# Starting addresses of matmul operands in SBUF: an FFT filter and a gated network on one core

## The chip, the core and the metric

The kernel runs on one core of a Trainium2 chip. A core has TensorE (matmuls; in the profile PE, and PEld for the loading of weights into its array), VectorE (DVE), ScalarE (ACT), GpSimd (POOL) and SyncE (SP), which here only issues DMAs. The engines compute on SBUF, a memory of 128 partitions in which an address is a byte within a partition, and TensorE writes its sums to PSUM. Data outside the core lies in HBM and is moved by 16 DMA engines. The metric is the time of one execution on the device in microseconds (us); lower is better.

## The reference

For 8 batches of 3136 x 256 the sequence axis is filtered through a real FFT, and the result goes through a small network with a gate:

```python
X = np.fft.rfft(x, axis=1)
Y = X * (filt_r + 1j * filt_i)[None]
y = np.fft.irfft(Y, n=3136, axis=1)               # (8, 3136, 256)
h = np.maximum(y @ w_in, 0.0)                     # w_in: 256 x 1024
hp = pad(h, one row of zeros before and behind)
conv_out = conv_w[0] * hp[0:S] + conv_w[1] * hp[1:S+1] + conv_w[2] * hp[2:S+2]
out = (h * sigmoid(conv_out)) @ w_out             # w_out: 1024 x 256
```

All inputs and the output are float32 or float64 on the host; the kernel computes in float32.

## The kernel before

The kernel has two stages, and each writes down by hand in which order its instructions go to TensorE, ScalarE, VectorE and GpSimd.

The first stage is the FFT filter. It is built of matmuls with tables (steps `first`, `second`, `filt`, `third`), and between the steps the data goes out to HBM and comes back in another order (`a_dram`, `b_dram`). It runs for all eight batches in one loop.

The second stage begins with the last step of the inverse transform, `last_stage` (line 216): four small matmuls with the table `m2_sb`, whose results `last_out` writes into the y tiles of the batch. y is kept transposed, the 256 channels in two groups of 128 partitions (KT = 2 rows of a tile) and the 3136 positions along the row, with one zero column before and one behind. To keep the precision of float32 in a faster matmul format (`F32R`), each value is split into a high part and a low part: `hi_act` (line 146, ScalarE) writes the rounded value, and `lo_dve` (line 149, VectorE) what is left of it. So each batch has two y tiles, y0 (high) and y1 (low), and each tile has two rows. Tiles of even batches come from the pool `y_even` at the right end of SBUF, those of odd batches from `y_odd` on the left. While the network runs on one batch, `last_stage` and `last_out` of the next batch are spread between its steps in 14 pieces.

The network runs in units. A chunk is 896 positions, halved into two parts of 448; for each of 28 chunks, of eight groups of 128 hidden channels (f) and of two halves (i) there is one unit, 448 in all:

- `inner` makes the hidden values of 450 positions (448 and a neighbour on either side). For each of the two rows `mm3` issues three matmuls: high weight by high value (line 177), high by low (178), low by high (179). The weights `wi[0]`, `wi[1]` are loaded into the array, and a window of the y row streams through. That makes six matmuls of 450 columns.
- `relu`, `conv`, `gate`, `split_g` (ScalarE, VectorE, GpSimd) take ReLU, the convolution over three positions and the gate, and split the result into two parts, g0 and g1.
- `project` multiplies g with `wo`: here g is loaded as weights, 128 positions at a time, and 256 columns of `wo` stream (lines 475 to 477), three matmuls for each of the chunk's seven groups of 128 positions: 12 matmuls for one half, 9 for the other.
- `evacuate` brings finished sums to `ot`, and SyncE issues their DMA.

Within a pool tiles lie one behind another, each beginning at a multiple of 32 bytes. Pools of the left side are stacked upwards, those of the right side (`side="right"`) downwards. The pool `wc` is the first on the left: it holds `m2_sb`, `cw` (the convolution's weights, 3 x 8 values for each partition), `wi0`, `wi1`, `wo0`, `wo1`. When the second stage begins, the first stage's tiles are given up, and `y_even`, `lp` (the inputs `br` of the last transform step), `y_odd` and `wp` (t, g, ot) are laid over them. A tile so placed waits for the last reader of the tile that lay there (`reuse_waits="tile"`).

Of the kernel before, what the change touches and what calls it, by code (L numbers as in the profile page):

```python
# [9 lines left out]
F32 = mybir.dt.float32  # L10
F32R = mybir.dt.float32r
# [5 lines left out]
S = 3136  # L17
# [5 lines left out]
KT = D // 128  # L23
NF = FF // 128
SUB = 448
NSUB = S // SUB
CH = 2 * SUB
NT = CH // 128


def _k1(g, s):
# [93 lines left out]
def tile_fft_filter_gated_ffn(  # L125
# [58 lines left out]

    wc = ctx.enter_context(tc.tile_pool(name="wc", bufs=1))
    m2_sb = wc.tile([112, N1], F32, name="m2_sb")
    cw = wc.tile([128, 3, NF], F32, name="cw")
    nc.gpsimd.memset(cw[:, 0, 0:1], 0.0)
    nc.scalar.activation(cw[:, 0, 0:1], cw[:, 0, 0:1], AF.Sigmoid)
    wi = [wc.tile([128, KT, FF], F32R, name=f"wi{h}") for h in range(2)]  # L190
# [3 lines left out]
    ys, yps = {}, []  # L194
# [6 lines left out]

    def y_slices(b, sl):
        if sl.start == 0:
            ys[b] = [yps[b % 2].tile([128, KT, S + 2], F32R, name=f"y{h}") for h in range(2)]
            for t in ys[b]:
                nc.gpsimd.memset(t[:, :, 0:1].bitcast(F32), 0.0)
                nc.gpsimd.memset(t[:, :, S + 1:S + 2].bitcast(F32), 0.0)
        return (t[:, :, 1:S + 1].rearrange("p k (a c) -> p k c a", c=N2)[:, :, sl] for t in ys[b])
# [19 lines left out]
    with (  # L228
# [17 lines left out]
        def load_filter(c):  # L246
            for e in (4 * c, 4 * c + 2):
                nc.sync.dma_start(out=t1_sb[0:64, e:e + 2], in_=fr[:, e:e + 2])
                nc.sync.dma_start(out=t2_sb[56:120, e:e + 2], in_=fi[:, e:e + 2])

        def copy_filter(c):
            sl = slice(4 * c, 4 * c + 4)
            nc.scalar.activation(t1_sb[64:120, sl], t1_sb[0:56, sl], AF.Copy)
            nc.scalar.activation(t2_sb[0:56, sl], t2_sb[64:120, sl], AF.Copy)
            if c == 6:
                nc.sync.dma_start(out=t1_sb[92:93, G - 1], in_=nyq)
# [3 lines left out]
        def load_weights(k):  # L260
            raws[k] = raw = cv.tile([128, 2, 512], I32, name="raw")
            for part, src in enumerate((w_in, w_out)):
                nc.sync.dma_start(out=raw[:, part], in_=src[:, 512 * k:512 * k + 512])
# [34 lines left out]
        def load(kind, b, p):  # L298
            r = pool(kind).tile([112, 2, D], F32, name=kind, bufs=8 if kind == "x" else 5)
            if kind == "x":  # L300
                v = x[b].rearrange("(p n) d -> p n d", n=N2)
            else:
                v = a_dram[b].rearrange("n (r g) d -> (n r) g d", g=G)
            nc.sync.dma_start(out=r, in_=v[:, 2 * p:2 * p + 2])
            rows[kind, b, p] = r

        def store(kind, b, p, ps):
            st = pool(kind).tile([112, 2, D], F32, name=kind, bufs=4)
            nc.scalar.activation(st, ps, AF.Copy)  # L309
            sl = slice(2 * p, 2 * p + 2)  # L310
            if kind == "sa":
                v = a_dram[b][sl].rearrange("n p d -> p n d")
            else:
                v = b_dram[b].rearrange("n (r g) d -> (n r) g d", g=G)[:, sl]
            nc.sync.dma_start(out=v, in_=st)

        def first(b, p):
            r = rows.pop(("x", b, p))
            ps = fps.tile([112, 2, D], F32, name="ps")
            for j in range(2):  # L320
                nc.tensor.matmul(ps[:, j], lhsT=s1_sb[:, 2 * p + j], rhs=r[:, j], start=True, stop=True)  # L321
            return ps

        def second(b, p):
            r = rows.pop(("a", b, p))
            pp = fps.tile([120, 2, D], F32, name="pp", bufs=3)
            if p < NP - 1:
                nc.tensor.matmul(pp, lhsT=s2_sb, rhs=r, start=True, stop=True)  # L328
            else:
                for j, m in ((0, s2_sb), (1, s2s_sb)):  # L330
                    nc.tensor.matmul(pp[:, j], lhsT=m, rhs=r[:, j], start=True, stop=True)
            psums[b, p] = pp

        def filt(b, p):


            pp, v = psums.pop((b, p)), turned[p % 2]
            sl = slice(2 * p, 2 * p + 2)
            u = fp.tile([120, 2, D], F32, name="u", bufs=3)
            nc.vector.tensor_mul(u, pp, t1_sb[:, sl])  # L340
            nc.vector.tensor_mul(v[64:120], pp[0:56], t2_sb[0:56, sl])
            nc.vector.scalar_tensor_tensor(out=v[0:56], in0=pp[64:120], scalar=-1.0, in1=t2_sb[64:120, sl], op0=ALU.mult, op1=ALU.mult)  # L342
            z = fp.tile([120, 2, D], F32, name="z", bufs=3)
            nc.gpsimd.tensor_tensor(out=z, in0=u, in1=v, op=ALU.add)  # L344
            parts["z", b, p] = z

        def third(b, p):
            z = parts.pop(("z", b, p))
            ps = fps.tile([112, 2, D], F32, name="ps")
            for j in range(2):  # L350
                nc.tensor.matmul(ps[:, j], lhsT=i1_sb[:, 2 * p + j], rhs=z[:, j], start=True, stop=True)  # L351
            return ps

        def at(i):
            return divmod(i, NP) if 0 <= i < NP * B else None
# [12 lines left out]
        with tc.manual_schedule(engines=COMPUTE):  # L368
            for i in range(NI):
                f, m = i, i - SKEW  # L370
                if i == done:
                    for _ in wsteps:
                        pass
                    forward_pools.close()
                    yps.append(ctx.enter_context(tc.tile_pool(name="y_even", bufs=1, side="right", reuse_waits="tile")))
                    lp = ctx.enter_context(tc.tile_pool(name="lp", bufs=2, side="right", reuse_waits="tile"))
                if 1 <= i < 4:
                    nc.sync.dma_start(out=s1_sb[:, 4 * i + 12:4 * i + 16], in_=s1[:, 4 * i + 12:4 * i + 16])
                if (bp := at(f + 7)) and i:
                    load("x", *bp)  # L380
                if bp := at(m + 3):
                    load("a", *bp)
                if i == 6:
                    nc.sync.dma_start(out=s2_sb, in_=s2[:, 0:120])
                    nc.sync.dma_start(out=s2s_sb, in_=s2s[:, 0:120])
                    nc.sync.dma_start(out=m2_sb, in_=m2)
                if 12 <= i < 26 and i % 2 == 0:
                    sl = slice((i - 12) // 2 * 4, (i - 12) // 2 * 4 + 4)
                    load_filter(i // 2 - 6)
                    nc.sync.dma_start(out=i1_sb[:, sl], in_=i1[:, sl])  # L390
                if bp := at(m - 2):
                    filt(*bp)
                pt = third(*bp) if (bp := at(m - 4)) else None
                pf = first(*bp) if (bp := at(f - 1)) else None
                if bp := at(m - 1):
                    second(*bp)
                if pt is not None:
                    store("sb", *at(m - 4), pt)
                if pf is not None:
                    store("sa", *at(f - 1), pf)  # L400
                if 3 <= i < 16:
                    next(csteps, None)
                if i == 16:
                    load_weights(0)
                    load_weights(1)
                if i >= 22:
                    next(wsteps, None)
                if 16 <= i < 30 and i % 2 == 0:
                    copy_filter(i // 2 - 8)
                c = 2 * (i - done)  # L410
                if 0 <= c - 4 < N2:
                    last_out(0, c - 4)
                if 0 <= c - 2 < N2:
                    last_stage(0, c - 2, fps.tile([128, 512], F32, name="ps"))
                if 0 <= c < N2:
                    last_load(0, c)
# [6 lines left out]

    outv = out.rearrange("b s d -> (b s) d").rearrange("(j t p) d -> j p t d", p=128, t=NT)
    hs, ts, gs, pos = {}, {}, {}, {}
# [39 lines left out]
    def project(j, f, i):  # L465
        gh, gl = gs[j, f]
        if f == 0 and i == 0:
            pos[j] = [ps_o.tile([128, 512], F32, name=f"po{k}") for k in range(4)], wp.tile([128, NT, D], F32, name="ot")
        po, ot = pos[j]
        tiles = range(4) if i == 0 else range(4, NT)  # L470
        for t in tiles:
# [7 lines left out]
    def evacuate(j, f, i):  # L479
# [4 lines left out]
        for k in (0, 1) if i == 0 else (2, 3):  # L484
            n = min(2, NT - 2 * k)
            o, src = ot[:, 2 * k:2 * k + n].rearrange("p t d -> p (t d)"), po[k][:, 0:n * D]
# [82 lines left out]
```

## Time and profile before

| | |
|---|---|
| Median of 3 runs | 1569.97 us (1563.34 to 1571.38) |
| The profiled execution, whole | 1563.82 us |
| Its span, from the first to the last instruction | 1562.0 us |
| TensorE's granted clock, mean over the span | 0.99 |
| First stage, limited by DMA | some 350 us |
| Second stage | some 1200 us |

How to read the lines of the profile: a group has its line of code, the engine, the operation, what it writes and reads (`ps_h<-y,wi` is a matmul that writes ps_h from y and the weights wi), the shape and the count; behind the bar busy microseconds in total and nanoseconds of one, and then the idle time before it. A line of the timeline has start, duration, engine, line and names. The duration of a matmul holds its way through the array and overlaps with the next one; the distance of two starts is what a matmul costs. Lines of waits have total microseconds, times, and the longest.

### The profile page before, as it was taken

The numbers are of one execution on the slowest core, as the hardware profiler recorded it, in microseconds if no ns is written. First come the engines' busy times: TensorE is split into PE (matmuls) and PEld (weight loads), VectorE is DVE, ScalarE is ACT, GpSimd is POOL, SyncE is SP. The second block draws the span as 40 slices with busy tenths as digits, with TensorE's granted clock in tenths as the row PEclk, the third lists the DMA queues.
The fourth block names the chain that finished last, engine by engine and source line by source line (L and its number), as shares of the span: only waits on it lengthen the run. The fifth ranks groups of instructions, "written<-read, shape, count | busy, mean of one in ns | idle before, by whom it ended". The sixth has DMA issues, their size and how long they took to land.

```text
span 1562.0 us, 26357 instructions
## 1 busy us (share of the span) xinstructions
PE 1503.0 (96%) x9424; PEld 1346.7 (86%) x9424; DVE 1280.6 (82%) x1965; ACT 1189.7 (76%) x2162; POOL 697.6 (45%) x624
## 2 busy tenths in 40 slices
PE   5799989998999999999999999999999999999998
PEld 3466656656999999999999999999999999999998
DVE  0578888888888888888888888888888888888887
ACT  3444444436888888888888888888888888888887
POOL 0356555643444444444444444444444444444444
PEclk9799999999999999999999999999999999999999
DMA  9999999993111011111110111111011110100001
GB/s 306 298 342 350 330 339 343 335 280 105 31 54 48 31 48 48 48 48 48 48 42 28 33 55 48 48 48 48 31 42 48 48 53 25 48 25 25 25 25 48
DMA packets 129397, 166.82 MB, mean 107 GB/s; under 512 B 10906, under 2 KB 87795, under 8 KB 129267
## 3 DMA queue, kind: packets, MB, share of 16 engines
q1 hardware_dynamic: 129267, 165.14, 32.8%
q8 instruction: 75, 1.23, 0.3%
q14 instruction: 55, 0.45, 0.1%
HBM read 88.03 MB, written 77.07 MB: 106 GB/s over the span
## 4 chain that ended last, share of the span: by engine, by line
PE 82%; DMA 12%; DVE 2%; SPq 1%; ACT 1%; issue 1%; POOL 0%; ACTq 0%; POOLq 0%
PE ps_h L178 12%; PE ps_h L179 12%; PE ps_h L177 11%; PE po L475 11%; PE po L477 11%; PE po L476 11%; PE ps_h L216 6%; DMA a<-a_dram 4%; DMA a_dram<-sa 3%; PE pp L328 3%; PE ps L351 2%; PE ps L321 2%; DMA b_dram<-sb 2%; DVE y L149 1%; ACT y L146 1%
## 5 line engine op out<-in xcount | busy, mean ns | idle before, releaser
L152 POOL TENSOR_TENSOR g<-t,g 128x448 fp32r<-128x448 f32 x448 | 517.5, 1155 | 668.2 <-ACT g L146 266.5
L475 PE MATMUL po<-wo,g 128*128 128x256 f32 x1568 | 441.5, 282 | 0.0
L477 PE MATMUL po<-wo,g 128*128 128x256 f32 x1568 | 433.8, 277 | 0.0
L476 PE MATMUL po<-wo,g 128*128 128x256 f32 x1568 | 433.4, 276 | 0.0
L449 DVE SCALAR_TENSOR_TENSOR t<-ps_h,cw,t 128x448 f32<-128x448 f32 x448 | 305.5, 682 | 82.8 <-ACT t L444 71.9
L178 PE MATMUL ps_h<-y,wi 128*128 128x450 f32 x896 | 330.4, 369 | 4.6 <-DVE y L149 4.6
L177 PE MATMUL ps_h<-y,wi 128*128 128x450 f32 x896 | 328.5, 367 | 3.2 <-DVE t L455 1.5
L179 PE MATMUL ps_h<-y,wi 128*128 128x450 f32 x896 | 328.6, 367 | 0.0
L450 DVE SCALAR_TENSOR_TENSOR t<-ps_h,cw,t 128x448 f32<-128x448 f32 x448 | 306.4, 684 | 16.0
L444 ACT ACTIVATE t<-ps_h,cw 128x448 f32<-128x448 f32 x448 | 285.1, 636 | 41.8 <-POOL g L152 0.4
L475 PEld LDWEIGHTS po<-wo,g 128*128 128x128 f32 x1568 | 294.7, 188 | 7.0
L476 PEld LDWEIGHTS po<-wo,g 128*128 128x128 f32 x1568 | 294.3, 188 | 5.7
L477 PEld LDWEIGHTS po<-wo,g 128*128 128x128 f32 x1568 | 294.4, 188 | 0.0
L442 ACT ACTIVATE ps_h<-ps_h 128x450 f32<-128x450 f32 x448 | 251.7, 562 | 31.8 <-PE ps_h L179 27.2
L455 DVE TENSOR_TENSOR t<-ps_h,t 128x448 f32<-128x448 f32 x448 | 275.1, 614 | 0.1
L454 ACT ACTIVATE t<-t 128x448 f32<-128x448 f32 x448 | 255.0, 569 | 12.1 <-DVE t L450 10.9
L146 ACT ACTIVATE g<-t 128x448 fp32r<-128x448 f32 x448 | 254.4, 568 | 0.2 <-DVE t L455 0.2
L344 POOL TENSOR_TENSOR z<-u,v 120x512 f32<-120x512 f32 x112 | 156.8, 1400 | 172.3 <-DVE v L342 162.9
L309 ACT ACTIVATE sb<-ps 112x512 f32<-112x512 f32 x112 | 66.8, 597 | 159.2 <-DMA b_dram<-sb 87.9
L179 PEld LDWEIGHTS ps_h<-y,wi 128*128 128x128 f32 x896 | 168.3, 188 | 13.9
L178 PEld LDWEIGHTS ps_h<-y,wi 128*128 128x128 f32 x896 | 168.3, 188 | 13.6 <-DVE y L149 6.8
L177 PEld LDWEIGHTS ps_h<-y,wi 128*128 128x128 f32 x896 | 169.9, 190 | 11.5 <-DVE t L455 2.6
(51 smaller groups left out, 1474.0 us busy)
## 6 DMA issues: line engine op xcount, KB each, us to landing
x<-in_x SPq DMA_DIRECT2D x112, 224.0 KB, 4.8
a_dram<-sa SPq DMA_DIRECT2D x112, 224.0 KB, 4.5
a<-a_dram SPq DMA_DIRECT2D x112, 224.0 KB, 4.7
b_dram<-sb SPq DMA_DIRECT2D x112, 224.0 KB, 4.5
br<-b_dram SPq DMA_DIRECT2D x112, 224.0 KB, 2.6
out<-ot SPq DMA_DIRECT2D x27, 896.0 KB, 4.1
raw<-in_w_in SPq DMA_DIRECT2D x8, 256.0 KB, 4.6
raw<-in_w_out SPq DMA_DIRECT2D x8, 256.0 KB, 5.6
```

The source lines that it names most:

```text
L146: nc.scalar.activation(dst, src, AF.Copy)
L152: nc.gpsimd.tensor_tensor(out=dst, in0=src, in1=hi.bitcast(F32), op=ALU.subtract)
L177: nc.tensor.matmul(ps, lhsT=wh, rhs=rh, start=start, stop=False, **kw)
L178: nc.tensor.matmul(ps, lhsT=wh, rhs=rl, start=False, stop=False, **kw)
L179: nc.tensor.matmul(ps, lhsT=wl, rhs=rh, start=False, stop=stop, **kw)
L444: nc.scalar.activation(t, h[:, 1:SUB + 1], AF.Copy, scale=cw[:, 1, f:f + 1])
L449: nc.vector.scalar_tensor_tensor(out=t, in0=h[:, 0:SUB], scalar=cw[:, 0, f:f + 1], in1=t, op0=ALU.mult, op1=ALU.add)
L450: nc.vector.scalar_tensor_tensor(out=t, in0=h[:, 2:SUB + 2], scalar=cw[:, 2, f:f + 1], in1=t, op0=ALU.mult, op1=ALU.add)
L455: nc.vector.tensor_mul(t, h[:, 1:SUB + 1], t)
L475: nc.tensor.matmul(o, lhsT=gh[:, sl], rhs=wo[0][:, f], start=first, stop=False, skip_group_check=True)
L476: nc.tensor.matmul(o, lhsT=gh[:, sl], rhs=wo[1][:, f], start=False, stop=False, skip_group_check=True)
L477: nc.tensor.matmul(o, lhsT=gl[:, sl], rhs=wo[0][:, f], start=False, stop=last, skip_group_check=True)
```

## The change

Four lines change, and only where tiles lie. The tile `cw` gets six rows in place of three, of which three are used. The rows of the y tiles get 3200 elements in place of 3138; the matmuls, the writes and the zero columns use the same elements as before. Ahead of the pool `y_even` a tile of 56 elements is laid at the right end, which nothing reads or writes.

```diff
+YROW = 3200
...
     m2_sb = wc.tile([112, N1], F32, name="m2_sb")
-    cw = wc.tile([128, 3, NF], F32, name="cw")
+    cw = wc.tile([128, 6, NF], F32, name="cw")[:, 0:3]
...
-            ys[b] = [yps[b % 2].tile([128, KT, S + 2], F32R, name=f"y{h}") for h in range(2)]
+            ys[b] = [yps[b % 2].tile([128, KT, YROW], F32R, name=f"y{h}") for h in range(2)]
...
                     forward_pools.close()
+                    pad = ctx.enter_context(tc.tile_pool(name="pad", bufs=1, side="right", reuse_waits="tile"))
+                    pad.tile([128, 56], F32, name="pad")
                     yps.append(ctx.enter_context(tc.tile_pool(name="y_even", bufs=1, side="right", reuse_waits="tile")))
```

## The prediction

> **What bounds the kernel now.** I read the 40 slices first, then the shares of busy time, the chain that ended last, the windows and the waits of the second stage, and last TensorE's own timeline, because a change of addresses can only act through the time that one instruction takes.
>
> ```profile
> PE 1503.0 (96%) x9424; PEld 1346.7 (86%) x9424; DVE 1280.6 (82%) x1965; ACT 1189.7 (76%) x2162; POOL 697.6 (45%) x624
> ...
> PE   5799989998999999999999999999999999999998
> ...
> PEclk9799999999999999999999999999999999999999
> DMA  9999999993111011111110111111011110100001
> ...
> PE 82%; DMA 12%; DVE 2%; SPq 1%; ACT 1%; issue 1%; POOL 0%; ACTq 0%; POOLq 0%
> ```
>
> The DMA row is full for nine slices (some 350 us): that is the transform stage, and its tiles are limited by transfers. From the tenth slice on PE is at 9 and DMA near 1: the gated network, 77% of the span. The chain gives PE 82%. In that second stage:
>
> ```profile
> 460.00:1562.00 1102.00, 1093.84 (x7620) 1050.79 (x7619) 933.46 (x1445) 950.62 (x1757) 484.32 (x443) 1.00 0.13 41
> ```
>
> (columns: length, then busy us of PE, PEld, DVE, ACT, POOL, then granted clock, DMA share, GB/s.) PE is busy 1093.84 of 1102 us at clock 1.00; DVE stands at 85% and ACT at 86%. So a nanosecond taken from a matmul's step is a nanosecond of the end, and there is room for some 14% before ACT would bind instead. What PE waits for there is small:
>
> ```profile
> PE ps_h L178 <- DVE y L149: 3.9, 7, 0.6
> ```
>
> Busy time and the recorded duration of one matmul are of no use here, since matmuls overlap. The start-to-start step is. One unit of work is six matmuls of 450 columns (y streams, wi stands), then 9 or 12 of 256 columns (wo streams, g stands):
>
> ```profile
> 400.05 0.37 PE L177 MATMUL ps_h<-y,wi 128*128 128x450 f32 x1
> 400.26 0.36 PE L178 MATMUL ps_h<-y,wi 128*128 128x450 f32 x1
> 400.46 0.37 PE L179 MATMUL ps_h<-y,wi 128*128 128x450 f32 x1
> 400.67 0.36 PE L177 MATMUL ps_h<-y,wi 128*128 128x450 f32 x1
> 400.87 0.37 PE L178 MATMUL ps_h<-y,wi 128*128 128x450 f32 x1
> 401.07 0.36 PE L179 MATMUL ps_h<-y,wi 128*128 128x450 f32 x1
> 401.28 0.28 PE L475 MATMUL po<-wo,g 128*128 128x256 f32 x1
> ...
> 402.30 0.37 PE L177 MATMUL ps_h<-y,wi 128*128 128x450 f32 x1
> ```
>
> Six steps take 1.23 us, and the nine of 256 columns 1.02 us, 0.113 each. The whole stage repeats this: of 442 complete sixes in the trace 433 last under 1.26 us, the first and the last of them being
>
> ```profile
> 388.37 0.37 PE L177 MATMUL ps_h<-y,wi 128*128 128x450 f32 x1
> ...
> 389.59 0.28 PE L475 MATMUL po<-wo,g 128*128 128x256 f32 x1
> ```
> ```profile
> 1548.40 0.37 PE L177 MATMUL ps_h<-y,wi 128*128 128x450 f32 x1
> ...
> 1549.63 0.28 PE L475 MATMUL po<-wo,g 128*128 128x256 f32 x1
> ```
>
> and over the 433 the mean steps, in order, are 205.0, 202.5, 205.8, 202.5, 207.5 and 204.7 ns (mean 204.7, the six 1228). The 256-column step is 113.25 ns. How many there are:
>
> ```profile
> L475 PE MATMUL po<-wo,g 128*128 128x256 f32 x1568 | 441.5, 282 | 0.0
> ...
> L178 PE MATMUL ps_h<-y,wi 128*128 128x450 f32 x896 | 330.4, 369 | 4.6 <-DVE y L149 4.6
> ```
>
> Three lines each: 2688 steps of 204.7 ns are 550 us, 4704 of 113.25 ns are 533 us. These two terms are 69% of the span, and all that the change touches.
>
> **The change part by part.**
>
> Addresses first, from the layout of the program. m2_sb begins at byte 16512 and takes 448, cw 96, so wi and wo begin at 17056 and after: 160 past a multiple of 256, and 32 past one of 64. All their slices are 512 or 1024 bytes apart, so this holds for every one. g begins 224 past. y0 (the high part) begins 160 past, y1 192 past, in both pools. The row of 3138 elements is 12552 bytes, 8 more than 49 x 256, so the second rows begin at 168 and 200. A matmul's window starts 1792 x u bytes into its row, which is 7 x 256 x u, so it keeps the row's offset. After the change cw takes 192 bytes and everything behind it begins at a multiple of 256; rows are 12800 = 50 x 256 bytes; 224 bytes of padding do the same for the right-hand side. t, g and ot have sizes that are multiples of 256, so they line up as well. The longer rows take 496 bytes more per tile, and the space is there.
>
> *Instructions.* None is added or removed: same matmuls, loads, DMAs, memsets (two columns per tile) and waits. The pad tile is never written, so nothing waits for it.
>
> *The moving rows (2688 steps).* The trace holds an experiment on this, because the six matmuls of a unit differ in nothing but addresses: start 160 gives 205.0 and 205.8, start 192 gives 202.5, start 168 gives 202.5 and 204.7, start 200 gives 207.5. The spread is 5 ns, and it isn't ordered by how well the start is aligned: a start that is 8 past a multiple of 16 (168) is as fast as one that is a multiple of 64 (192). Each row ends the same way too: 1800 bytes touch 8 blocks of 256, 29 of 64 and 113 of 16 from every one of these starts, and from an aligned one. Bounds: all six as the slowest, +2.8 x 2688 = +7.6 us; all as the fastest, -2.2 x 2688 = -5.8 us. I take -5.8, since of the rows seen the start at 192 is the nearest to a multiple of 256.
>
> [...]
>
> *The weights (PEld).* A weight load lies under the matmul before it. In the six it is hidden with room: recorded durations are
>
> ```profile
> L475 PEld LDWEIGHTS po<-wo,g 128*128 128x128 f32 x1568 | 294.7, 188 | 7.0
> ```
>
> 188 ns with its latency, against a step of 205. In the 256-column steps it may not be hidden. The nearest row is the last transform step, which has the same 128 columns of weights but streams only 112:
>
> ```profile
> 845.09 1.04 PE L216 MATMUL ps_h<-m_sb,br 112*128 112x112 f32 x8
> ```
> ```profile
> L216 PE MATMUL ps_h<-m_sb,br x784: 259/275/363, 391.9 to 1396.2; 112*128 112x112 f32 x196
> ```
>
> Eight in 1.04 us with 0.275 for the last one: (1.04 - 0.275) / 7 = 0.109 us each. What the stream alone would need comes from the half-pace matmuls of the first stage:
>
> ```profile
> 100.36 1.03 PE L321 MATMUL ps<-x,s_sb 112*112 112x256 f32 x4
> ```
> ```profile
> L321 PE MATMUL ps<-x,s_sb 112*112 112x256 f32 x356 | 93.2, 384 | 0.0
> ```
>
> (1.03 - 0.384) / 3 = 0.215 us for 256 columns at half pace, so 0.42 ns a column at full pace (my estimate): 107.6 ns for 256 columns and 189.2 for 450. So a load of 128 columns paces at 109 and the stream at 108; which of the two makes the 113.25 can't be told. Does alignment shorten the load? No load in the trace starts on a multiple of 64 or 256, but two offsets are there (br at 160, g at 224) with 109 and 113. Bounds: -5.7 x 4704 = -27 us if the step falls to what the stream needs, 0 if the pace isn't the load's or doesn't hang on the address. I take 0: nothing in the rows shows an address at work there.
>
> *Other engines.* DVE and ACT write y with a stride of 28 elements, and only the distance between its two rows changes:
>
> ```profile
> L146 ACT ACTIVATE y<-ps_h 128x448 fp32r<-128x448 f32 x89 | 94.3, 1059 | 66.3 <-PE ps_h L216 66.3
> L149 DVE TENSOR_TENSOR y<-ps_h,y 128x448 fp32r<-128x448 f32 x89 | 93.6, 1052 | 71.0 <-ACT y L146 71.0
> ```
>
> Should each become 10% dearer, that is 0.1 us x 89 on engines with 14% idle; all of it on PE would be 9 us, all of the present wait (3.9 us) gone -4. I take 0. The t and g tiles move for ACT, DVE and POOL, behind the same idle shares.
>
> *Where the stages meet.* y_odd and the tiles behind it lie over other old tiles of the transform than before (shifted by up to 1 KB), so first uses may wait for other readers. Between 360 and 460 us PE is idle for 6 us; I take 0, with 1 us either way. Transfers of the first stage keep their order and sizes: 0.
>
> **Sum:** -5.8 us, which on the profiled execution (span 1562.0, 1563.82 in all) is 1558.0. That execution lies 6 us under the median of the runs shown (1569.97; they reach from 1563.34 to 1571.38). I take the middle of 1558 and 1570 - 5.8 = 1564: 1561 us.
>
> **The rivals.**
>
> *A, faster: one of the two losses hangs on the address.* The 450-column step has 204.7 - 189.2 = 15.5 ns over its stream, the 256-column step 5.7. If aligned weights let the second run at its stream, -27 us. If aligned rows bring the first to the same small loss as the second, -(15.5 - 5.7) x 2688 = -26 us. Either gives about 1537. For it: the 15.5 ns need a cause, and column count alone is a poor one (450/256 x 5.7 is 10). Against: wo streams from 160 past 256, exactly as y0 does, with a third of the loss; and the six offsets seen differ by only 5 ns. Half the gain counts here as well.
>
> *B, faster still: both losses vanish,* -(15.5 x 2688 + 5.7 x 4704) = -68 us, 1495. [...]
>
> *C, slower: weight load and stream collide.* When all operands begin at the same offset, a load and the stream beside it start on the same place modulo 256, where now they are 0 to 64 bytes apart. Price: the slowest start seen, 207.5, is the floor (+7.6 us); twice its distance from the mean is +15 us, 1579. It decides once the mean of the six passes 207.6 ns. For it: the slow step is a fact without an explanation. Against: y0 and wi already share the offset 160, and that step is at 205.0. Far bound: were the load's 188 ns bare in each 256-column step, +75 x 4704 = +350 us; no row points there.
>
> *D, the addresses don't come out as said* (a tile placed otherwise): then time stays, 1564 to 1570. It falls together with my forecast.
>
> **How the numbers follow.** About 0.5%, 8 us, is what a measurement of this kernel can tell from no change. Forecast with D 0.52; A 0.29, B 0.05; C 0.14. A at half its gain (-13) still counts as faster. So faster 0.34, same 0.52, slower 0.14. The range must take in the forecast, most of A and the near end of C: 1531 to 1577. The forecast's own range is 1553 to 1571.
>
> **What would show it.** The steps in TensorE's timeline: by my forecast the six become alike, 1.215 us together and no longer 1.228, and the 256-column step stays 0.113. A shows as a six of 1.17 or a step of 0.108; B as both; C as a six of 1.25 or more. If the steps stay and the time moves, I am wrong about where addresses act: then the y writes, the first stage's 350 us or the meeting of the stages have changed, and the windows show which.

## The result, and the profile after

The changed kernel takes 1591.48 us (median of 4 runs, 1590.53 to 1593.38) against 1569.4 us before: a ratio of 1.0149, with a 95% interval of 1.0119 to 1.0178. It is slower by some 22 us. The forecast, 1561 us, was wrong, and the time lies above its range of 1531 to 1577.

From the page of the changed kernel: busy time of the engines, then one group of the 256-column matmuls and one of the 450-column matmuls (lines have moved on by one to three).

```profile
PE 1524.1 (96%) x9424; PEld 1374.6 (87%) x9424; DVE 1280.8 (81%) x1965; ACT 1192.1 (75%) x2162; POOL 697.8 (44%) x624
...
L478 PE MATMUL po<-wo,g 128*128 128x256 f32 x1568 | 451.0, 288 | 0.0
...
L179 PE MATMUL ps_h<-y,wi 128*128 128x450 f32 x896 | 328.4, 367 | 4.5 <-DVE y L150 4.5
```

The window of the second stage and its waits, in the same columns as before:

```profile
460.00:1562.00 1102.00, 1097.95 (x7481) 1060.09 (x7480) 921.18 (x1425) 938.98 (x1731) 474.81 (x435) 1.00 0.13 41
```
```profile
PE ps_h L179 <- DVE y L150: 3.8, 7, 0.6
```

The instructions, the clock (1.00) and PE's wait (3.8 us) are as they were. PE is busy throughout, yet fewer of its matmuls fit into the same 1102 us: 7481 and no longer 7620. So single matmuls have become longer, and the group of 256 columns shows it (288 ns recorded, 282 before), the one of 450 doesn't. TensorE's timeline of the changed kernel, one unit (start, duration):

```profile
1151.52 0.37 PE L178 MATMUL ps_h<-y,wi 128*128 128x450 f32 x1
1151.72 0.36 PE L179 MATMUL ps_h<-y,wi 128*128 128x450 f32 x1
1151.93 0.37 PE L180 MATMUL ps_h<-y,wi 128*128 128x450 f32 x1
1152.13 0.36 PE L178 MATMUL ps_h<-y,wi 128*128 128x450 f32 x1
1152.33 0.37 PE L179 MATMUL ps_h<-y,wi 128*128 128x450 f32 x1
1152.54 0.36 PE L180 MATMUL ps_h<-y,wi 128*128 128x450 f32 x1
1152.74 0.28 PE L478 MATMUL po<-wo,g 128*128 128x256 f32 x1
...
1153.70 0.28 PE L480 MATMUL po<-wo,g 128*128 128x256 f32 x1
1153.82 0.37 PE L178 MATMUL ps_h<-y,wi 128*128 128x450 f32 x1
```

Six steps take 1.22 us, the nine of 256 columns 1.08 us, 0.120 each. Over the whole stage (434 of 442 sixes undisturbed, and all runs of 9 or 12 steps that don't follow a last transform step) the six are 1221.5 ns (before 1228.1) and the 256-column step 119.8 ns (before 113.25). That accounts for the result:

- 4704 x 6.57 ns = +30.9 us
- 448 x -6.6 ns = -3.0 us
- the first matmul of the network starts at 376.97 us, before at 373.74: +3.2 us. In the runs below it lies anywhere between 373 and 381 us, and the control that moves no offset has 375.5; I put it down to the first stage's own variation.
- the 98 runs of 256-column steps behind a last transform step were slowed by less than the 6.57 ns for each step, some 30 ns a run less (their first step is 201.7 ns before and 202.7 after): -2.9 us

Together +28.2 us against 26.7 us between the two spans; most of the rest lies in steps of 450 columns, which gained some 1 us more than the -3.0 counted here. All 256-column steps added up, start to start, became 27.9 us longer, so the loss sits wholly in them, where g is loaded and wo streams. (The two medians differ by less than the two spans because the profiled execution of the kernel before, 1563.82 us, is near the fastest of its runs.)

### The profile page after: what moved, and what is told of

The parts are those of the page before. It is cut to its first block, busy times and chain, and to the rows that moved or that the text cites. A ratio compares the mean times of both kernels' runs of the same rounds, so it can differ in the third digit from the quotient of the medians.

```text
span 1588.8 us, 26357 instructions
## 1 busy us (share of the span) xinstructions
PE 1524.1 (96%) x9424; PEld 1374.6 (87%) x9424; DVE 1280.8 (81%) x1965; ACT 1192.1 (75%) x2162; POOL 697.8 (44%) x624
## 4 chain that ended last, share of the span: by engine, by line
PE 82%; DMA 11%; DVE 3%; SPq 2%; ACT 1%; issue 1%; POOL 0%; ACTq 0%; POOLq 0%
PE po L478 12%; PE po L479 12%; PE po L480 12%; PE ps_h L179 11%; PE ps_h L180 11%; PE ps_h L178 11%; PE ps_h L217 5%; DMA a<-a_dram 4%; PE pp L329 3%; DMA a_dram<-sa 3%; PE ps L352 2%; PE ps L322 2%; DMA x<-in_x 1%; DMA b_dram<-sb 1%; DVE y L150 1%
## 5 line engine op out<-in xcount | busy, mean ns | idle before, releaser
L478 PE MATMUL po<-wo,g 128*128 128x256 f32 x1568 | 451.0, 288 | 0.0
L479 PE MATMUL po<-wo,g 128*128 128x256 f32 x1568 | 443.3, 283 | 0.0
L480 PE MATMUL po<-wo,g 128*128 128x256 f32 x1568 | 443.0, 283 | 0.0
L479 PEld LDWEIGHTS po<-wo,g 128*128 128x128 f32 x1568 | 299.3, 191 | 4.8
L478 PEld LDWEIGHTS po<-wo,g 128*128 128x128 f32 x1568 | 298.6, 190 | 5.2
L480 PEld LDWEIGHTS po<-wo,g 128*128 128x128 f32 x1568 | 299.8, 191 | 0.0
```

Of the source, the lines that this page charges most:

```text
L478: nc.tensor.matmul(o, lhsT=gh[:, sl], rhs=wo[0][:, f], start=first, stop=False, skip_group_check=True)
L479: nc.tensor.matmul(o, lhsT=gh[:, sl], rhs=wo[1][:, f], start=False, stop=False, skip_group_check=True)
L480: nc.tensor.matmul(o, lhsT=gl[:, sl], rhs=wo[0][:, f], start=False, stop=last, skip_group_check=True)
```

## The experiments

Steps in this section are means in ns of the same kind as above, from the start times in each run's timeline; offsets are bytes past a multiple of 256. The means repeat within 0.1 ns where a run has the same offsets as the kernel before (`all_256` below), so one execution is enough to tell layouts apart by their steps, though its time varies by several us. "Behind a six" means all runs of 9 or 12 steps that follow six 450-column matmuls directly; the steps given are those. In the kernel before, wi and wo lie at 160, g at 224 and the four y rows at 160, 168 (high), 192, 200 (low); in the changed one everything lies at 0.

### One operand back

`g_back`: g, and ot behind it, back at 224.

```diff
         if i == 0:
+            if (j, f) == (0, 0):
+                wp.tile([128, 56], F32, name="gpad", bufs=1)
             gs[j, f] = [wp.tile([128, 2 * SUB], F32R, name=f"g{h}", bufs=4) for h in range(2)]
```

> The changed kernel with 224 bytes of padding ahead of the g tiles alone, so that g starts 224 past a multiple of 256 as before; wo stays at 0. In the changed kernel the 256-column step went from 113.25 to 119.8 ns (4704 of them, +31 us), while the six of 450 columns went from 1228 to 1221.5 ns. Theory LOAD (a weight load of g that starts on a multiple of 256 is dearer): 113.25 again, some 31 us less than the changed kernel, about 1560. Theory STREAM (wo streaming from a multiple of 256 is dearer): 119.8 stays, about 1591. Theory PAIR (what counts is the distance of the two starts, 64 before, 0 after, 224 here): neither follows of itself, but not 119.8 unless 224 is as bad as 0.

`w_back`: wi and wo back at 160, the rest kept at 0.

```diff
-    cw = wc.tile([128, 6, NF], F32, name="cw")[:, 0:3]
+    cw = wc.tile([128, 3, NF], F32, name="cw")
...
     wo = [wc.tile([128, NF, D], F32R, name=f"wo{h}") for h in range(2)]
+    wc.tile([128, 24], F32, name="wpad")
```

> The changed kernel with wi and wo back at 160 past a multiple of 256; y, t, g and ot stay at 0. LOAD: the 256-column step stays at 119.8 ns. STREAM: 113.25. PAIR: the distance of g from wo is 96, so below 119.8. For the six of 450 columns: if the 6.6 ns gained came from y alone, 1221.5 stays; if from the weights wi, 1228.

Measured: `g_back` 116.9 ns and 1579.91 us; `w_back` 117.4 ns and 1591.47 us (kernel before beside them: 1566.45). Neither undoes the loss and both undo some of it, so neither LOAD nor STREAM holds. The six in `w_back` became 1240.5, worse than in either kernel; in `g_back`, where nothing of the six moved but the load of g beside its last matmul, they went from 1221.5 to 1226.9, most of it in the second step (206.6, in the changed kernel 202.5).

### Many distances in one kernel

`grid` and `grid2` lay the slices of wi and wo 1056 or 544 bytes apart, and g in four buffers with offsets of their own. The lines are those of `grid2`; in `grid` every g tile is 16 elements longer and the rows of y are 3216 long.

```diff
+FW = 128 + 8
+DW = D + 8
...
-    wi = [wc.tile([128, KT, FF], F32R, name=f"wi{h}") for h in range(2)]
-    wo = [wc.tile([128, NF, D], F32R, name=f"wo{h}") for h in range(2)]
+    wi = [wc.tile([128, KT, NF, FW], F32R, name=f"wi{h}") for h in range(2)]
+    wo = [wc.tile([128, NF, DW], F32R, name=f"wo{h}") for h in range(2)]
...
-            gs[j, f] = [wp.tile([128, 2 * SUB], F32R, name=f"g{h}", bufs=4) for h in range(2)]
+            n = (f + j) % 4
+            gs[j, f] = [wp.tile([128, 2 * SUB + 16 * h], F32R, name=f"g{h}{n}", bufs=1)[:, 0:2 * SUB] for h in range(2)]
```

> Many offsets in one kernel, same computation: slices f of wi and wo lie at 32 x f past a multiple of 256, the g buffers at 0 and 64 or 128 and 192 (high and low part, in turn), the four y rows at 0, 64, 128 and 192. LOAD: steps group by g's offset alone. STREAM: by wo's alone, whatever g. PAIR: by the distance of the two, with 120 ns where it is 0 and 113 where it is 64. The whole time says little, since every case is mixed: between 1560 and 1590.

> A grid without mixed cases: slices f of wi and wo at 32 x f past a multiple of 256, high and low part of g at the same offset, 0, 64, 128 or 192 in turn, all y rows at multiples of 256. PAIR: the mean 256-column step depends on the distance g - wo alone, so the same step on every diagonal of the table; 120 ns at 0, 113.3 at 64. If single offsets count: rows or columns of the table are alike, not diagonals. The six of 450 columns: by distance y - wi, 1221.5 at 0.

`grid`, with high and low part of g at different offsets, has 116.6 to 119.2 in all its cells: too mixed to read (1589.49 us). `grid2` (1588.07 us) reads well. Mean step of each cell:

| wo at | g at 0 | g at 64 | g at 128 | g at 192 |
|---|---|---|---|---|
| 0 | 119.3 | 115.8 | 118.5 | 117.5 |
| 32 | 117.2 | 118.2 | 118.6 | 119.9 |
| 64 | 117.6 | 119.8 | 116.7 | 118.0 |
| 96 | 119.5 | 117.0 | 118.4 | 117.7 |
| 128 | 119.1 | 117.5 | 119.2 | 115.9 |
| 160 | 118.3 | 119.5 | 117.1 | 118.2 |
| 192 | 114.9 | 118.2 | 114.7 | 119.6 |
| 224 | 117.6 | 118.3 | 119.5 | 116.7 |

Rows and columns are not alike; diagonals are. Distance g - wo of 0: 119.2 to 119.8. Of 160: 119.5 to 119.9. Of 64: 114.9 to 116.7. Of 224: 116.7 to 117.2. The eight distances account for 83% of the variance between the cells, the eight offsets of wo for 12% and the four of g for none. So the distance counts, not the offset of either operand. But the diagonal at 64 isn't at 113.25, and 192 spreads from 114.7 to 117.6, so the distance isn't all that counts.

### Does a multiple of 256 matter at all?

`yrow_only` takes from the change the long rows alone, `cw_only` the padded cw alone (the two diffs are those of the change). `all_256` is the control.

```diff
+    wc.tile([128, 64], F32, name="wpad")
     m2_sb = wc.tile([112, N1], F32, name="m2_sb")
```

> The kernel before with the longer y rows alone. wi and wo stay 160 past a multiple of 256, both rows of y move to 160 (odd batches) and 224 (even), and the longer tiles push t, g and ot on to 160, so g and wo lie at the same offset, and nothing at a multiple of 256. PAIR (the distance g - wo modulo 256 counts): 119.8 ns for the 256-column step and about 1590 us, as in the changed kernel. MULTIPLES (a start on a multiple of 256 is what costs): 113.3 and about 1566.

> The kernel before with the padded cw alone. wi and wo begin at multiples of 256, g at 64, y of odd batches at 0, 8, 32 and 40, y of even batches stays at 160, 168, 192 and 200. MULTIPLES: 119.8 ns. PAIR: the distance g - wo is 64 as before, so 113.3 ns, 1563 to 1570 us; with the second state that the grid shows at this distance (117.7 ns in some units), depending on how the six before ends, up to 118.

> Control: the kernel before with 256 bytes of padding at the very start, so that every tile on the left keeps its offset modulo 256 and all lie 256 further on. If offsets modulo 256 are all that counts: 1228 ns for the six, 113.25 for the 256-column step, 1563 to 1570 us. If higher address bits count: other steps, as in the run with wo and g put back (118.0, where the distance was 64 modulo 256 and yet not 113.3).

Measured: `yrow_only` 119.8 ns in odd batches and 119.5 in even, 1586.43 us; `cw_only` 113.25 ns, 1572.37 us; `all_256` 113.25 ns, six 1228.0, 1564.62 us (before: 1565.55). The timeline of `yrow_only`:

```profile
1154.44 0.28 PE L476 MATMUL po<-wo,g 128*128 128x256 f32 x1
...
1155.52 0.37 PE L178 MATMUL ps_h<-y,wi 128*128 128x450 f32 x1
```

Nine steps in 1.08 us, as in the changed kernel, though none of y, wi, wo and g begins at a multiple of 256 there. In `cw_only` wi and wo do begin there, and nothing is lost in the steps behind a six; its timeline:

```profile
1154.49 0.28 PE L475 MATMUL po<-wo,g 128*128 128x256 f32 x1
...
1155.51 0.37 PE L177 MATMUL ps_h<-y,wi 128*128 128x450 f32 x1
```

Nine steps in 1.02 us, as in the kernel before. (Behind a last transform step, whose operand br isn't moved along, the runs of `cw_only` settle near 113 or near 118.) That settles the multiples. The long rows alone bring the loss: they push g from 224 to 160, the offset of wo.

In odd batches `cw_only` has every operand 160 below where it is before, and repeats its six to 0.2 ns: 205.2, 202.5, 205.8, 202.5, 207.5, 204.6.

### Both operands back, and the same distance elsewhere

`proj_back` puts wo at 160 and g at 224 and leaves wi and y at 0. `g64` is the changed kernel with g at 64. `w_g_back` has wi and wo at 160, g at 224 and only y at 0. All have distance 64.

```diff
+    wc.tile([128, 40], F32, name="wpad0")
     wo = [wc.tile([128, NF, D], F32R, name=f"wo{h}") for h in range(2)]
+    wc.tile([128, 24], F32, name="wpad1")
...
+                wp.tile([128, 56], F32, name="gpad", bufs=1)      (g64: 16 in place of 56, and no wpad)
```

> The changed kernel with both operands of the 256-column steps back where they were before (wo 160, g 224 past a multiple of 256), wi and y at multiples of 256. Moving g alone back gave steps of 116.9 ns and moving wo alone back 117.4, in runs of four or five different steps, so neither operand alone is the cause. PAIR (the distance of the two starts counts): 113.3 ns again, and the loss of 31 us is gone: 1560 to 1565. If instead something else that moved with them counts (t, ot, y behind them): not 113.3.

> The changed kernel with 64 bytes of padding ahead of g: distance g - wo 64 as before, wi, wo and y at multiples of 256. PAIR alone: 113.3 ns and about 1562 us. PAIR with two states: 113.3 or 117.7, settled by how the six hands over to the first 256-column step, and the same in every unit, since all units are alike here.

> The changed kernel with wi, wo (160) and g (224) all back, so that only y is still at multiples of 256 (before: 160, 168, 192, 200). The distance g - wo is 64, as in the run with wo and g put back, which nevertheless had 118.0 ns. HANDOVER (at distance 64 there are two states, and the end of the six settles which): another result than 118.0 is possible though g and wo stand as there, 113.3 or a mixture; STRICT PAIR (the distance alone): 118.0 can't be explained by it, nor any difference from it here. The six: w_back had 1240 with the same wi and y; if the six hangs on the state handed over, it is other than 1240.

Measured: `proj_back` 117.9 ns, 1585.05 us; `g64` 115.5, 1573.83 us; `w_g_back` 115.0 with sixes of 1248.3, 1582.79 us. The strict form of PAIR falls: one distance, four results. (Modulo 512 the distance is 64 in `g64` and the kernel before and 320 in the other two. That doesn't explain the difference: `w_g_back` settles at 113.3 like `g64`, and `y_224` below has two results at 64 modulo 512.) `g64` differs from the changed kernel in the place of g and ot alone, and ot is written only once in eight units, so it is g's place that makes the difference. What `g64` does can be seen in its timeline:

```profile
1101.58 0.28 PE L480 MATMUL po<-wo,g 128*128 128x256 f32 x1
1101.70 0.28 PE L481 MATMUL po<-wo,g 128*128 128x256 f32 x1
1101.82 0.28 PE L482 MATMUL po<-wo,g 128*128 128x256 f32 x1
1101.94 0.28 PE L480 MATMUL po<-wo,g 128*128 128x256 f32 x1
1102.05 0.28 PE L481 MATMUL po<-wo,g 128*128 128x256 f32 x1
...
1102.62 0.37 PE L178 MATMUL ps_h<-y,wi 128*128 128x450 f32 x1
```

Steps of 0.12 at first, then (1102.62 - 1102.05) / 5 = 0.114: the mean steps are 122.5, 117.5, 119.2, 115.8, 114.2, and from there 113.4. The step falls into a rhythm, and how soon depends on what ran before. In `proj_back` it stays in another rhythm, near 117.7, behind a six; but its 98 runs behind a last transform step, with the same offsets of g and wo, reach 113.3 by their sixth step. Of the versions at distance 64, all others but `y_224` below settle at 113.3 behind a six.

### Trying to steer the start

Three versions with g and wo where they are before and only y moved: `yrow_g224` has all rows at 160, `y_224` all at 224, and `y1_160` keeps the high part at 160 and 168 and moves the low part there too.

```diff
-            ys[b] = [yps[b % 2].tile([128, KT, S + 2], F32R, name=f"y{h}") for h in range(2)]
+            ys[b] = [yps[b % 2].tile([128, KT, YROW], F32R, name=f"y{h}") for h in range(2)]     (yrow_g224, y_224; YROW = 3200)
+            ys[b] = [yps[b % 2].tile([128, 6336], F32R, name=f"y{h}")[:, 0:KT * (S + 2)].rearrange("p (k s) -> p k s", k=KT) for h in range(2)]     (y1_160)
```

Not shown are the tiles of padding that put y, and g where it needs it, at the offsets named.

> A version meant to beat both: the kernel before with the longer y rows, y at 160 in both pools (the offset of wi), and 64 bytes ahead of g so that g - wo is 64. The six should be near 1222 (distance 0 of y and wi, as in the odd batches of the run with the longer rows alone), the 256-column step 113.3 if the handover leads to the fast state: 448 x -6 ns = -3 us against the kernel before, 0.2%, so not to be told from no change; with the slow state 118: +20 us.

> The kernel before with longer y rows and all y rows at 224, so 64 from wi (160), as g from wo. If the distance of a weight load from the stream beside it counts in the six as in the 256-column steps: near 1219 ns, as in the even batches of the run with the longer rows alone. The 256-column steps 113.3 with a fast or a slow start: 1560 or 1570.

> The kernel before with only the low part of y moved, by 32 bytes: both y tiles begin at 160, their second rows at 168; wi, wo at 160 and g at 224 as before. HANDOVER (how the last matmul of the six, which streams the second row of the high part, meets the first load of g settles the state of the 256-column steps): that matmul stands as before, so 113.3 ns from the first step on, and not the slow start of 122, 118, 119, 116, 114 ns that came when this row moved to 160; about 1560 to 1570. If the start is slow again, 1570 or more.

| run | y rows at | six | first steps of 256 columns | mean step | time |
|---|---|---|---|---|---|
| before | 160, 168, 192, 200 | 1228.1 | 112.5, 113.4, 113.4 | 113.25 | 1566.7 (beside `yrow_g224`), 1567.43 (beside the others) |
| `yrow_g224` | 160 | 1223.2 | 122.5, 117.5, 119.2 | 115.5 | 1573.22 |
| `y1_160` | 160, 168 twice | 1237.7 | 124.0, 115.9, 114.2 | 114.7 | 1578.12 |
| `y_224` | 224 | 1236.3 | two kinds | 115.6 | 1577.26 |

No version beats the kernel before: `yrow_g224`, with 6 executions against 11, has a ratio of 1.0044 to it (1.0029 to 1.0058), slower by some 7 us. In `y_224` the sixes, expected near 1219 from the even batches of `yrow_only`, are 1236.3, though y and wi lie as they do there; of the operands of these matmuls g alone lies elsewhere. The guess that the last matmul of the six settles the start fell with `y1_160`, where that matmul's row stands as before. And `y_224` shows two rhythms with the same offsets in one execution:

```profile
1102.72 0.28 PE L477 MATMUL po<-wo,g 128*128 128x256 f32 x1
...
1103.74 0.36 PE L178 MATMUL ps_h<-y,wi 128*128 128x450 f32 x1
```
```profile
1111.55 0.28 PE L477 MATMUL po<-wo,g 128*128 128x256 f32 x1
...
1112.96 0.37 PE L178 MATMUL ps_h<-y,wi 128*128 128x450 f32 x1
```

Nine steps in 1.02 us are 0.113 each, twelve in 1.41 are 0.1175. Of its 343 runs of 9 or 12 steps behind a six, 172 settle near 113 and 171 near 118. The order isn't chance: of 342 pairs of neighbouring runs with only a six between them, 341 have one run near 113 and one near 118. The sixes alternate too: the first step of a six is 200 ns behind a run near 113 and 206 behind one near 118. So the same offsets allow two rhythms here, and what one run hands over through the six decides which the next one falls into. What is handed over, a time or something else, isn't shown.

`g64` and `yrow_g224` have all offsets but a common 160 in common. Their sixes are the same to 0.1 ns (205.0, 202.5, 204.2, 202.5, 204.2, 205.8 where the 256-column steps follow), and the first five steps behind them agree to 0.1 ns too. Together with `all_256` and the odd batches of `cw_only` that is the third case: moving y, wi, wo and g together changes nothing.

### What the load has to do with it

`half_stream` cuts each 256-column matmul in two of 128 columns, each with its full load. `half_load` and `quarter_load` load 64 and 32 of the 128 columns of g in the changed kernel and leave the streams whole; the other output positions are left out.

```diff
+            sl, o = slice(128 * t, 128 * t + 64), o[0:64]                       (half_load; quarter_load: 32)
             nc.tensor.matmul(o, lhsT=gh[:, sl], rhs=wo[0][:, f], start=first, ...
...
+            for q in range(2):                                                  (half_stream)
+                c, oq = slice(128 * q, 128 * q + 128), o[:, 128 * q:128 * q + 128]
+                nc.tensor.matmul(oq, lhsT=gh[:, sl], rhs=wo[0][:, f, c], ...
```

> The changed kernel with each 256-column matmul made as two of 128 columns, each with the whole load of 128 columns: 9408 steps. This measures the load's own pace: if a load of g at a multiple of 256 takes 112 ns as that of the last transform step does (there 128 columns of weights and 112 streamed, 112 ns before and after the change), the step is 107 to 113 and the load alone doesn't make the 119.8; if it is 118 to 120, the load alone makes it. Time about 1590 + 4704 x 100 ns = 2060 us.

> The changed kernel with 64 columns of weights in place of 128 in every 256-column step, the streams unchanged; half of the output positions is left out (zeros). CONFLICT (the load slows the stream, or waits for it, while both read SBUF): the step falls from 119.8 ns, about half way to the stream's own 108, to 113 or less. If the step is the stream's alone and has nothing to do with the load: 119.8 stays.

> The changed kernel with 32 columns of weights in place of 128 in every 256-column step, the streams whole; three quarters of the output positions are left out (zeros). With 64 columns the step settled at 113.3 after two slow ones. CONFLICT: 113.3 from the start or below; if it stays at 113.3, that is the stream's own floor with a change of weights, and the kernel before had nothing left to gain there by addresses; towards 108: the load cost 5 ns in the kernel before, too. If the load had no part in it: 119.8.

`half_stream`: 111.65 ns a step from the second on, 2072.67 us. Here the load sets the pace, with g at 0 (the first step of a run is 61 ns, so 128 columns of stream need no more), and it is no dearer than the 112 ns of the last transform step, which is the same in both kernels. `half_load`: 114.0 (112.5, 117.5, 116.7, then 113.3), 1566.63 us. `quarter_load`: 117.2, wandering between 114.2 and 120.0, 1582.51 us; its timeline:

```profile
1153.35 0.28 PE L480 MATMUL po<-wo,g 128*32 128x256 f32 x1
...
1154.40 0.38 PE L178 MATMUL ps_h<-y,wi 128*128 128x450 f32 x1
```

Nine steps in 1.05 us, 0.117 each, with a quarter of the load. So the load matters (a shorter one gives other steps at the same offsets), but not by the share of time or bytes that it takes: full 119.8, half 114.0, quarter 117.2. The simple picture, in which the load takes reading time from the stream in proportion to its size, doesn't fit the last one. A matmul with fewer columns of weights also writes fewer partitions of its result, and no run separates the two. As in `g64`, the step settles in a rhythm, and which one can't be read off the size of the load.

## Why the prediction was wrong

**What bounds the kernel** was right: the second stage follows PE's steps one to one (the steps of 256 columns 27.9 us longer, the sixes 3.0 shorter, the spans 26.7 apart), and DVE and ACT never came to bind (921.18 and 938.98 us busy of 1102 in the changed kernel, PE 1097.95).

**The moving rows.** Forecast -5.8 us; measured -3.0 us (448 x -6.6 ns). The sign was right, the reason not, so the sign was luck: the gain doesn't come from alignment. With y at the offset of wi, and g at that of wo, the six are 1221.5 at 0 and 1222.4 at 160 (odd batches of `yrow_only`); with y at 0 and wi at 160 they are 1240.5 to 1248.3. My bounds of -5.8 and +7.6 us, from the six offsets in the trace, held only for that arrangement.

**The weights in the 256-column steps.** This is the step that failed. I bounded it by -27 us and 0 and took 0, since "nothing in the rows shows an address at work there". It was +27.9 us (6.57 ns on each of 4704 would be 30.9). The rows couldn't show it: before, g and wo have one distance, 64, in every one of the 4704 steps, so the trace held no experiment on it, and I read its silence as proof that no cost was possible. One thing they did show and I passed over: behind a last transform step the second to fourth of these steps take 121.6, 115.8 and 114.2 ns in the kernel before, with operands at the same distance, so the step hung on more than the columns loaded and streamed. I also looked at the load's own start (br at 160, g at 224) where the distance from the stream beside it counts (119.2 to 119.8 ns at 0 and 114.9 to 116.7 at 64 in `grid2`). One term of that paragraph was rough: the 109 ns for br averages seven steps, of which the first is 99 and the third to seventh are 111.7. And 107.6 and 189.2 ns are estimates that take the float32 matmuls of the first stage for half as fast as those of the second. At a granted clock of 0.50 the kernel before shows that factor: four float32 steps of 256 columns from 53.78 to 55.49 us, 427 ns each, and six steps of 450 columns from 375.42 to 377.67 us, 375 ns each, are 1.67 and 0.83 ns a column. At 1.00 it doesn't: 215 ns against 113.25 for 256 columns is a factor of 1.9, and the shortest steps of its second stage, 112 ns for 256 columns and 202 for 450, stay above both estimates.

**Rival C** (weight load and stream collide at equal offsets) named the right pair and the right sign, with a chance of 0.14. Its price was wrong: I put it into the 450-column steps (+7.6 to +15 us), where equal offsets cost nothing (the six 1221.5 ns, before 1228.1), and had only a far bound for the 256-column steps. So its sign, a six of 1.25 us or more, didn't show (1.22). A "collision" as I described it isn't shown either, as `quarter_load` says (117.2 ns with a quarter of the load, 114.0 with half). My argument against it, that y0 and wi share an offset at 205.0 ns, was one pair of operands taken for another.

**Rivals A and B** (a loss goes) fell: the six stood at 1221.5 ns, and the 256-column step rose to 119.8. **D** didn't happen: the offsets came out as said. **Other engines, and where the stages meet**: nothing showed beyond the variation of the first stage.

Load and stream aren't without effect on each other here. A quarter of the load doesn't give the shortest step (117.2 ns), half of it does shorten it (114.0 against 119.8), and the step depends on where the loaded tile lies relative to the streamed one (113.25 ns at a distance of 64 in the kernel before, 119.8 at 0 in the changed one). By what path is open.

What stays open is what keeps the rhythm. The settled means are near 113.3 (the kernel before), 116.7 (`g_back`), 117.5 (`y_224`) and 120.0 ns (the changed kernel), and the single steps (112.5, 113.3, 114.2 and 115.8 in the kernel before, 116.7 in `half_load`, 117.5 and 119.2 in `g64`, 120.0 in the changed kernel) are all close to multiples of 0.83 ns; a pattern repeats after one step (the changed kernel) to five (`g_back` and `w_back` have four or five), and a common shift of y, wi, wo and g changes nothing (`all_256`: 113.25 ns and 1228.0, before 113.25 and 1228.1). I didn't find the state that is handed from one run of matmuls to the next, and so can't say beforehand which rhythm a layout gives.

## What to carry to other kernels

Where TensorE reloads weights for every matmul and its steps set the time, the distance modulo 256 between the loaded tile and the streamed one was worth up to 6% of a 256-column step here (113.25 ns at 64, 119.8 at 0), and a change of a tile's size upstream can shift it, as the long rows did in `yrow_only` (119.8 and 119.5 ns); so after such a change compare steps from the timeline, not busy time. Alignment to 256 by itself is worth nothing here (`cw_only`, wi and wo at 0: 113.25 ns, as before). A short step also doesn't carry over from one layout to another at the same distance, because what ran before it counts too (at a distance of 64: 113.25 ns in the kernel before, 115.5 in `g64`, 117.9 in `proj_back`). A trace in which a quantity never varies says nothing on what varying it costs: give such a term a bound on both sides.

## What the runs showed of the hardware

- The step of a 256-column matmul with its own load of 128 columns lies between 113.25 (the kernel before) and 119.8 ns (the changed one) on average at the same clock (1.00), by the distance of the two operands (in the cells of `grid2` 119.2 to 119.8 at distance 0, 114.9 to 116.7 at 64) and by what ran before (at distance 64 again 117.9 in `proj_back`).
- There is memory in it: with the same offsets in one execution 172 runs of steps settle near 113 ns and 171 near 118, and the two kinds alternate in 341 of 342 neighbouring pairs (`y_224`).
- Moving y, wi, wo and g by the same amount (by 256 bytes in `all_256`, to offsets 160 lower in the odd batches of `cw_only`) leaves the steps of the six and those behind a six as they were, to 0.2 ns.
- Where the load sets the pace, 128 columns of it take 111.65 ns with g at 0 (`half_stream`) and 111.7 with br at 160 (the kernel before) and at 0 (the changed one). 32 columns of load in place of 128 (117.2 ns) don't give the shortest step; 64 (114.0) come closer to it.
